# Casting loads for chunk 0's q and v and all of chunk 1, masks spread by VectorE, and preparation steps one slot later, in a fused attention and MLP kernel

## The chip, the cores and the metric

The kernel runs on one core of one Trainium2 chip. The metric is the device time of one execution in microseconds (us), lower is better. TensorE (PE) multiplies, VectorE (DVE) and ScalarE (ACT) work elementwise and empty PSUM, GpSimd (POOL) builds masks, casts, and issues the DMAs that convert types on the way, SyncE (SP) issues plain DMAs.

## What is computed

Causal attention over 4 batches, 8 heads, 768 positions, head size 64. Heads 0, 2 and 6 see all earlier positions; the others see the first 4 positions (the sinks) and the last 64. Its output, with the heads side by side, goes through a two-layer MLP.

```python
stream_keep = causal & (is_sink | in_win)
mask = np.where(retr, full_mask, stream_mask)
scores = np.where(mask, scale * np.matmul(q, k.transpose(0, 1, 3, 2)), -1e9)
a = softmax(scores)
x = np.matmul(a, v).transpose(0, 2, 1, 3).reshape(B * S, H * D)   # 3072 x 512
h = x @ w_in                                                      # 512 x 2048
out = np.maximum(0.01 * h, h) @ w_out                             # 2048 x 512
```

## The kernel before

The 3072 token rows are cut into eight **chunks** of 384, two for each batch. Every chunk n goes through four stages:

- **Load**: q, k and v as bf16, `qb`, `kb`, `va`. `load(n)` does this with casting DMAs from POOL's queue, three for each of q, k and v (one for each 128 tokens, 1024 pieces of 64 numbers). Chunk 0 and chunk 1's q and k are instead staged as fp32 in tiles `f` by `load_wide` and cast by an engine; a piece there is three tokens of a head, so that tokens come out in the order 3p+g, and the copies behind the transposes put them back (`WIDE = 2`).
- **Preparation** (`prep_pair(n, p)` for a pair p of heads, `prep_half` in chunk 0): six PE transposes into one PSUM bank, two copies to `kt` (on DVE), one to `qt`.
- **Attention** (`Attention(n)`): eight heads, each a score step (`qk`: PE, exp on ACT, mask on DVE) and a value step (`av`), then `finish` (DVE, to `xs`) and `x_t` (PE transposes through the bank `pt`, ACT copy to `xt`). Heads with a window read values shifted by 64 positions, `vb`: in chunk 0's first batch made on PE (`v_shift_pe`), otherwise by two SBUF copies by DMA (`v_shift`, L184, L185).
- **MLP**: sixteen input ticks (`in_slots`: four matmuls of 384 columns, L452, and an activation on ACT) and sixteen output slots (`out_slots`: three tiles of 128 tokens, L465, a DVE copy L470 and an output DMA from SP).

The order on every engine is that of the program text (`manual_schedule`). `merge` spreads one list of steps among another: the MLP of chunk n runs among the attention of n+1 and the preparation of n+2. `Attention.slots` hangs a preparation step (`extra`) behind the slot in which a pair's `x_t` runs. The prologue is written out by hand: constants, chunk 0's preparation and attention, chunk 1's preparation, then the first input ticks; `v_shift(3)` is issued from ACT's queue behind the MLP of chunk 1.

PSUM has eight banks: `ph`, `psS` and `po` two each, `py` and `pt` one each. POOL's DMAs use eight semaphores in turn, so an issue waits until the eighth before it has landed; POOL's other work waits behind it.

Of the kernel before, what the change touches and what calls it, by code (L numbers as in the profile page):

```python
# [21 lines left out]
def kernel(  # L22
# [46 lines left out]
    def load_wide(n, nm, half, eng):  # L69

        if half != 1:
            stage[nm, n] = rot.tile([128, 3 * H * D], FP32, name="f", tag="f", bufs=5)
            if nm != "v":
                cast[nm, n] = rot.tile([128, 3, H, D], BF16, name=f"{nm}b", tag=f"{nm}b", bufs=2)
        t = stage[nm, n]
        if nm == "v":
            for g in range(3):
                eng.dma_start(out=v_src(n)[:, g], in_=nat[nm][0, n, :, :, g])
            return
        hs = slice(0, H) if half is None else slice(4 * half, 4 * half + 4)  # L80
        eng.dma_start(out=t.rearrange("p (h x) -> p h x", h=H)[:, hs], in_=wide[nm][0, n, :, hs])

    def qk_src(nm, n):
        return stage[nm, n].rearrange("p (h g d) -> p g h d", h=H, g=3)

    def v_src(n):
        return stage["v", n].rearrange("p (g h d) -> p g h d", g=3, h=H)
# [49 lines left out]
    def zeros(i):  # L137
        nc.vector.memset(kt[i][64:128, :, 0, :], 0.0)
        nc.vector.memset(kt[i][0:64, :, 1, :], 0.0)
        nc.gpsimd.memset(va[i][:, :, :, D], 1.0)  # L140
        nc.gpsimd.memset(ksink[i][:], 0.0)
        nc.gpsimd.memset(vs[i][:, 0, :], 0.0)

    def constants():
        make_identity(nc, ident)
# [2 lines left out]
        nc.gpsimd.memset(m_win[:], 1.0)
        keep(m_win[:], [[0, 6], [-1, 64]], ALU.is_gt, 0, 1)
        keep(m_win[:], [[0, 6], [1, 64]], ALU.is_ge, 64, -1)  # L150

        nc.gpsimd.memset(shift[:], 0.0)
        nc.gpsimd.memset(e_sink[:], 0.0)
        zeros(0)
# [347 lines left out]
    constants()  # L502
    ktb, qtb = cast["k", 0], cast["q", 0]
    lo, hi = slice(0, 4), slice(4, 8)
    k0, q0, v0 = qk_src("k", 0), qk_src("q", 0), v_src(0)
# [21 lines left out]
    load_wide(1, "k", None, nc.gpsimd)
    load_wide(1, "q", None, nc.gpsimd)
    sink_mask()
    nc.gpsimd.tensor_copy(va[0][:, 0, :, 0:D], v0[:, 0])  # L530
    nc.gpsimd.tensor_copy(va[0][:, 2, :, 0:D], v0[:, 2])
    for i in range(4):
        load_w("in", i)
    load(1, "v")
    for i in range(4):
        load_w("out", i)
# [97 lines left out]
```

## Time and profile before

| what | value |
|---|---|
| median of three runs (lowest to highest) | 277.66 us (277.31 to 278.5) |
| the profiled execution: its time / its span from the first to the last instruction | 277.87 / 276.2 us |
| PE busy | 239.3 us, 87% |
| DVE, ACT, POOL busy | 112.9, 140.1, 69.9 us |

PE is busy for 87% of the span, but not evenly: the page's slices show it near full behind the first third and with holes before it. So the profile is read by stretch: when PE stood still, and who released it. The timeline gives each instruction's start and length and, in brackets, the idle time before it with the engine that ended it; the waits are the same idle times summed by the two lines.

### The profile page before, as it was taken

The page shows a single profiled execution, that of the slowest core. Times are in us where ns is not written, and L with a number is a line of the kernel's source. Part 1 is how long each engine was busy: PE and PEld are TensorE (multiplying, and loading weights), DVE is VectorE, ACT ScalarE, POOL GpSimd, SP SyncE. Part 2 cuts the span into 40 slices and gives each one's busy share as a digit, 9 for nine tenths or more (in the row PEclk, how much of TensorE's full clock was granted, in tenths as well). Part 3 has the DMA queues.
Part 4 walks back from the last instruction along what each step waited for, and adds up shares of the span by engine and source line. Part 5 has one row for each costly group of instructions (what it writes and reads, how often), then busy time and mean ns, then how long its engine had stood idle before and what let it go on. Part 6 is the DMA issues. An engine that isn't in the chain of part 4 may idle for free.

```text
span 276.2 us, 5264 instructions
## 1 busy us (share of the span) xinstructions
PE 239.3 (87%) x2135; PEld 147.3 (53%) x2164; DVE 112.9 (41%) x303; ACT 140.1 (51%) x304; POOL 69.9 (25%) x101
## 2 busy tenths in 40 slices
PE   1661669988869988979999999999999999999995
PEld 1451435545446545655666566665665566555544
DVE  6772351135363554454354524553563124311012
ACT  3652157744537327765555466655554766633300
POOL 5693936710056047009100820000000000000000
PEclk9998599999999999999999999999999999999999
DMA  6899999991249139909901992102110211011122
GB/s 215 192 250 206 188 220 160 149 101 40 77 28 143 43 55 168 84 2 93 125 34 40 96 168 44 40 4 75 38 42 29 69 38 40 0 40 39 38 78 76
DMA packets 73865, 24.63 MB, mean 89 GB/s; under 512 B 63249, under 2 KB 69649, under 8 KB 73841
## 3 DMA queue, kind: packets, MB, share of 16 engines
q0 software_dynamic: 63888, 13.24, 56.8%
q1 hardware_dynamic: 9152, 9.32, 10.4%
q10 hardware_dynamic: 800, 1.73, 2.5%
q8 instruction: 17, 0.28, 0.5%
q14 instruction: 8, 0.06, 0.1%
HBM read 27.26 MB, written 6.29 MB: 122 GB/s over the span
## 4 chain that ended last, share of the span: by engine, by line
PE 72%; DMA 9%; DVE 8%; POOL 4%; ACT 3%; issue 2%; SPq 0%; ACTq 0%; DVEq 0%
PE ph L452 26%; PE py L465 26%; PE po L287 5%; DMA w_in_bf<-in_moe_w_in_dram 4%; PE psS L329 4%; DVE kt L230 3%; PE psS L465 3%; PE pt L220 3%; DMA f<-in_k_dram 3%; DMA vb<-va 3%; PE pt L405 2%; DVE o L470 2%; PE psS L365 2%; PE psS L309 1%; DVE qt L230 1%
## 5 line engine op out<-in xcount | busy, mean ns | idle before, releaser
L452 PE MATMUL ph<-xt,w_in_bf 128*128 128x384 bf16 x512 | 102.8, 327 | 2.6 <-ACT xt L406 1.6
L454 ACT ACTIVATE g<-ph 128x384 bf16<-128x384 f32 x128 | 62.7, 491 | 61.3 <-PE ph L452 61.0
L465 PE MATMUL py<-w_out_bf,g 128*128 128x512 bf16 (+1 forms) x324 | 86.9, 373 | 3.7 <-DVE o L470 2.2
L452 PEld LDWEIGHTS <-w_in_bf 128*128 128x128 bf16 x512 | 45.6, 98 | 30.2 <-issue 4.1
L465 PEld LDWEIGHTS <-g 128*128 128x128 bf16 x400 | 35.3, 97 | 27.6 <-issue 4.0
L334 ACT ACTIVATE at<-psS 128x384 bf16<-128x384 f32 x82 | 39.6, 490 | 15.5 <-PE psS L329 14.6
L97 POOL DMA_DIRECT2D kb<-in_k_dram x18 | 15.8, 890 | 72.9 <-PE pt L220 72.5
L470 DVE COPY o<-py 128x512 f32<-128x512 f32 (+1 forms) x22 | 14.9, 678 | 32.2 <-PE py L465 32.1
L329 PE MATMUL psS<-qt,kt 128*128 128x384 bf16 (+2 forms) x105 | 26.9, 296 | 0.0
L230 DVE COPY kt<-pt 64x384 bf16<-64x384 bf16 x48 | 17.0, 355 | 18.3 <-PE pt L220 17.7
L374 DVE TENSOR_TENSOR ats<-ats,m_win 128x384 bf16<-128x384 bf16 x40 | 14.6, 365 | 20.3 <-ACT ats L370 20.0
L370 ACT ACTIVATE ats<-psS 128x384 bf16<-128x384 f32 x37 | 18.0, 490 | 9.6 <-PE psS L365 9.6
L340 DVE TENSOR_TENSOR at<-at,m_caus 128x128 bf16<-128x128 bf16 x24 | 5.4, 225 | 39.2 <-ACT at L334 39.1
L406 ACT ACTIVATE xt<-pt 128x384 bf16<-128x384 bf16 x31 | 15.2, 489 | 11.3 <-PE pt L405 10.8
L287 PE MATMUL po<-va,at 128*128 128x65 bf16 x237 | 20.0, 196 | 0.6 <-DVE at L338 0.4
L287 PEld LDWEIGHTS <-at 128*128 128x128 bf16 x252 | 16.3, 100 | 6.4 <-DVE at L338 1.0
L97 POOL DMA_DIRECT2D va<-in_v_dram x21 | 18.7, 927 | 3.0 <-DMA w_out_bf<-in_moe_w_out_dram 2.9
L399 DVE TENSOR_TENSOR xs<-po,linv 128x384 bf16<-128x384 f32 x31 | 17.3, 558 | 1.1
L97 POOL DMA_DIRECT2D qb<-in_q_dram x18 | 15.9, 910 | 4.1 <-DMA w_out_bf<-in_moe_w_out_dram 3.5
L220 PEld LDWEIGHTS <-kb 128*128 128x128 bf16 x84 | 7.0, 101 | 17.5 <-POOL kb L539 7.9
L365 PEld LDWEIGHTS <-kt 128*128 128x128 bf16 x240 | 12.5, 102 | 5.3
L287 PEld LDWEIGHTS <-ats 128*128 128x128 bf16 x240 | 11.6, 98 | 5.5 <-issue 1.8
(104 smaller groups left out, 221.6 us busy)
## 6 DMA issues: line engine op xcount, KB each, us to landing
out_dram<-o SPq DMA_DIRECT2D x23, 256.0 KB, 2.0
va<-in_v_dram POOLq DMA_DIRECT2D x21, 128.0 KB, 7.7
kb<-in_k_dram POOLq DMA_DIRECT2D x18, 128.0 KB, 4.8
qb<-in_q_dram POOLq DMA_DIRECT2D x18, 128.0 KB, 6.8
w_in_bf<-in_moe_w_in_dram POOLq DMA_DIRECT2D x4, 512.0 KB, 9.6
w_out_bf<-in_moe_w_out_dram POOLq DMA_DIRECT2D x4, 512.0 KB, 16.3
vb<-va ACTq DMA_DIRECT2D x6, 195.0 KB, 6.2
f<-in_k_dram SPq DMA_DIRECT2D x2, 384.0 KB, 5.3
```

The lines of the kernel that those rows point to most:

```text
L97: nc.gpsimd.dma_start(out=o, in_=nat[nm][b, c, :, :, g])
L230: nc.vector.tensor_copy(dst, src)
L287: nc.tensor.matmul(o, lhsT=lhsT, rhs=rhs, start=first, stop=False, skip_group_check=True)
L329: nc.tensor.matmul(s[:, off : off + w], lhsT=kt[i][:, p, hh, 128 * kj : 128 * kj + 128], rhs=qts[n][:, p, lo:CH], start=(j == 0), stop=(j ...
L334: nc.scalar.activation(out=a[:, 0:off], in_=s[:, 0:off], func=ACTF.Exp, scale=SM)
L365: nc.tensor.matmul(s[:, 64 * m : 64 * m + 64], lhsT=kt[i][:, p, hh, k0 : k0 + 128], rhs=qts[n][:, p, 64 * m : 64 * m + 64], start=(m == 0) ...
L370: nc.scalar.activation(out=av_, in_=s[:, 0:CH].rearrange("p (j e f) -> p j e f", j=3, e=2), func=ACTF.Exp, scale=SM)
L399: nc.vector.tensor_tensor(xs[:], po[:, :, :, 0:D], linv.to_broadcast([128, 3, 2, D]), op=ALU.mult)
L452: nc.tensor.matmul(ph[:, 0:CH], lhsT=w_in_bf[:, g, 128 * t : 128 * t + 128], rhs=xts[n][:, g, :], start=(g == 0), stop=(g == KG - 1))
L454: nc.scalar.activation(out=gs[n][:, t, :], in_=ph[:, 0:CH], func=ACTF.Prelu, alpha=0.01)
L465: nc.tensor.matmul(py[n][:, 0 : c1 - c0], lhsT=gs[n][:, ng, 128 * tt : 128 * tt + 128], rhs=w_out_bf[:, ng, c0:c1], start=(ng == 0), stop= ...
L470: nc.vector.tensor_copy(o[:, 0 : c1 - c0], py[n][:, 0 : c1 - c0])
```

## The change

- `load_wide` is gone. Chunk 0's k still comes as fp32, from SP in two halves (`load_k0`); chunk 0's q and v and all of chunk 1 come by `load`, in POOL's queue ahead of the weights. POOL's casts go, and so do ACT's casts of q; the second half of chunk 0's k is cast on ACT instead of on POOL. With `WIDE = 1` the copies of chunk 1's preparation are plain (both orders now put the same tokens in the same columns).
- POOL builds the window mask and the sink mask at 64 and 8 columns (`m_w`, `m_h`); DVE spreads them in `late_constants`, which stands behind chunk 0's second half of the preparation now. The zero fills of `shift`, `e_sink`, `ksink` and `vs` go from POOL to DVE.
- In chunk 0, S5's scores come behind R0's value step, and R6's second score step behind `finish(1)`. Chunk 1's second and third preparation change banks; its fourth comes behind one input tick instead of two.
- An `extra` comes one slot further behind `x_t` (`LAG + 3`). Chunk 1's output tiles take the banks `py`, `ph`, `py`. `v_shift(3)` is issued from SP right behind `v_shift(2)`, with all of `load(3)` at one place.

```diff
-    WIDE = 2
+    WIDE = 1
...
-    for half in range(2):
-        load_wide(0, "k", half, nc.sync)
-        load_wide(0, "q", half, nc.sync)
-    load_wide(0, "v", None, nc.sync)
+    load_k0(0)
+    load_k0(1)
...
     def late_constants():
...
+        nc.vector.tensor_copy(m_win[:], spread(m_w[:], 6, 64))
+        nc.vector.tensor_copy(m_win0[:, 1:], spread(m_w[:], 5, 64))
...
+                nc.vector.memset(m_h[:, h : h + 1], 0.0)
+        nc.vector.tensor_copy(m_sink[:], m_h[:].rearrange("p (h o) -> p h o", o=1).to_broadcast([128, H, D + 1]))
...
         def move(e, dst, src):
-            if n < WIDE:
-
-                src = src.rearrange("p g t -> p t g")
-                dst = dst.rearrange("p (t g) -> p t g", g=3)
-            else:
-                dst = dst.rearrange("p (g t) -> p g t", g=3)
+            dst = dst.rearrange("p (g t) -> p g t", g=3)
...
-                if extra and t in (extra_at or [last[p] + LAG + 2 for p in range(4)]):
+                if extra and t in (extra_at or [last[p] + LAG + 3 for p in range(4)]):
...
+    make_identity(nc, ident)
+    load(0, "q")
+    masks()
+    for t in va:
+        nc.gpsimd.memset(t[:, :, :, D], 1.0)
+    load(0, "v")
+    nc.vector.memset(shift[:], 0.0)
+    nc.vector.memset(e_sink[:], 0.0)
+    zeros(0)
+    load(1, "kq")
     for i in range(4):
         load_w("in", i)
     load(1, "v")
     for i in range(4):
         load_w("out", i)
-    for nm in "kq":
-        for g in range(3):
-            nc.gpsimd.tensor_copy(cast[nm, 1][:, g], qk_src(nm, 1)[:, g])
...
+    qk(*R0)
+    prep_half(0, 1, ("po", "po"),
+              lambda: nc.scalar.activation(out=cast["k", 0][:, :, 4:8], in_=k0[:, :, 4:8], func=ACTF.Copy),
+              lambda: None)
     load(2)
-    load(3, "kq")
+    late_constants()
...
-    run(in0[2:12])
+    run(in0[1:11])
     zeros(1)
-    load(3, "v")
+    load(3)
...
     v_shift(2, nc.sync)
+    v_shift(3, nc.sync)
     load(4)
     in1 = in_slots(1)
-    run(in1[0:4])
-    run(merge(in1[4:] + out_slots(1), preps(2) + Attention(2).slots(preps(3))))
-    v_shift(3)
+    run(in1[0:2])
+    run(merge(in1[2:] + out_slots(1, ("py", "ph", "py")), preps(2) + Attention(2).slots(preps(3))))
```

**POOL, from the masks to chunk 2's k.** Before, with chunk 1's q and k as wide loads to `f` and their casts behind the weights' issues:

```order
L525 CAST kb<-f 128x3x256
L81 DMA f<-in_k_dram 128x8x192
L81 DMA f<-in_q_dram 128x8x192
L169 MEMSET m_sink 128x520
L134 AFFINE_SELECT m_sink<-m_sink 128x520 x2
L174 MEMSET m_sink 128x65 x3
L530 CAST va_87<-f 128x8x64
L531 CAST va_87<-f 128x8x64
L103 DMA w_in_bf<-in_moe_w_in_dram 128x4x512 x4
L97 DMA va_87<-in_v_dram 128x8x64 x3
L106 DMA w_out_bf<-in_moe_w_out_dram 128x4x512 x4
L539 CAST kb<-f 128x512 x3
```

After, from the identity on (the first `qb` is chunk 0's, the `kb` and `qb` behind `va_79` chunk 1's):

```order
L85 DMA qb<-in_q_dram 128x8x64 x3
L133 MEMSET m_caus 128x128
L120 AFFINE_SELECT m_caus<-m_caus 128x128
L135 MEMSET m_w 128x64
L120 AFFINE_SELECT m_w<-m_w 128x64 x2
L139 MEMSET m_h 128x8
L120 AFFINE_SELECT m_h<-m_h 128x8 x2
L85 DMA va_79<-in_v_dram 128x8x64 x3
L85 DMA kb<-in_k_dram 128x8x64 x3
L85 DMA qb<-in_q_dram 128x8x64 x3
L91 DMA w_in_bf<-in_moe_w_in_dram 128x4x512 x4
```

No cast is left behind the issues of `w_out_bf`, whose waits for landings POOL must sit out; chunk 1's q and k stand ahead of all weights.

**DVE, from chunk 0's second half of `kt` to the first masked window head.** Before:

```order
L261 COPY kt_85<-po 64x2x384
L210 COPY ksink_93<-kt_85 64x4
L261 COPY kt_85<-po 64x2x384
L210 COPY ksink_93<-kt_85 64x4 x2
L374 TENSOR_TENSOR ats_95<-ats_95,m_win_81 128x3x2x64
```

After:

```order
L195 COPY ksink_85<-kt_77 64x4 x2
L148 COPY shift<-ident 128x64
L149 COPY shift<-ident 128x64
L150 COPY e_sink<-ident 128x32
L152 COPY m_win<-m_w 128x384
L153 COPY m_win_73<-m_w 128x320
L154 COPY m_win_73<-m_caus 128x64
L155 MEMSET m_win_73 4x64
L158 MEMSET m_h 128x1 x3
L159 COPY m_sink<-m_h 128x520
L355 TENSOR_TENSOR ats_87<-ats_87,m_win_73 128x3x2x64
```

Eleven instructions for constants moved in between; six of them stood ahead of the first cast of k before.

**SP, around the outputs of chunk 0** (`vb1` is the second batch's shifted v; the pair of 1040 is `v_shift(2)`, the pair of 1560 `v_shift(3)`). Before:

```order
L471 DMA out_0_dram<-o_668 128x512
L471 DMA out_0_dram<-o_742 128x512
L471 DMA out_0_dram<-o_877 128x512
L184 DMA vb1_90<-va1_88 64x1040
L185 DMA vb1_90<-va1_88 64x1040
L471 DMA out_0_dram<-o_1165 128x512
```

After:

```order
L452 DMA out_0_dram<-o_871 128x512
L169 DMA vb1_82<-va1_80 64x1040
L170 DMA vb1_82<-va1_80 64x1040
L169 DMA vb1_82<-va1_80 64x1560
L170 DMA vb1_82<-va1_80 64x1560
L452 DMA out_0_dram<-o_1182 128x512
```

The pair of 1560 came from ACT's queue, where it stood behind all of chunk 1's MLP.

## Rows read from the trace of the kernel before

**Rows 1.** The page's 40 slices of 6.9 us: busy tenths of PE

```profile
PE   1661669988869988979999999999999999999995
```

**Rows 2.** Stretches: us, busy PE, PEld, DVE, ACT, POOL (instructions), granted clock, DMA

```profile
10.00:22.00 12.00, 9.14 (x109) 6.62 (x109) 8.41 (x24) 7.93 (x18) 11.45 (x18) 1.00 1.00 227
22.00:29.00 7.00, 0.16 (x3) 0.09 (x1) 0.59 (x2) 0.49 (x1) 2.99 (x5) 0.72 1.40 199
29.00:41.00 12.00, 8.15 (x63) 5.50 (x64) 6.22 (x11) 4.47 (x10) 7.83 (x11) 0.74 1.38 208
...
129.00:276.20 147.20, 142.45 (x1200) 86.07 (x1219) 51.63 (x138) 75.13 (x163) 10.87 (x13) 1.00 0.39 56
```

**Rows 3.** PE's timeline: start, length, operation, in brackets the idle time before

```profile
21.73 0.34 PE L405 MATMUL py<-ident,xs 128*128 128x128 bf16 x3
28.91 0.29 PE L220 MATMUL ph<-ident,kb 128*128 128x128 bf16 x1 [6.84 <-POOL kb L539]
...
31.67 0.29 PE L220 MATMUL ph<-ident,qb 128*128 128x128 bf16 x1 [0.27 <-POOL qb L539]
...
40.63 1.46 PE L452 MATMUL ph<-xt,w_in_bf 128*128 128x384 bf16 x8 [0.88 <-ACT g L454]
...
53.97 1.03 PE L465 MATMUL py<-w_out_bf,g 128*128 128x512 bf16 x4
```

**Rows 4.** POOL's timeline: constants, and issues of the weights' loads

```profile
1.08 0.29 POOL masks.py:199 TENSOR_SCALAR_AFFINE_SELECT ident<-ident 128x128 bf16<-128x128 bf16 x1
...
4.47 0.16 POOL L142 MEMSET vs<- 128x65 bf16 x1
...
15.25 3.02 POOL L103 DMA_DIRECT2D w_in_bf<-in_moe_w_in_dram  x4
...
27.50 0.74 POOL L106 DMA_DIRECT2D w_out_bf<-in_moe_w_out_dram  x1 [1.76 <-DMA w_in_bf<-in_moe_w_in_dram]
```

**Rows 5.** PE's waits: us in total, times, longest

```profile
PE pt L220 <- DVE qt L230: 3.3, 4, 0.9
PE py L465 <- DVE o L470: 2.2, 4, 0.6
...
PE po L287 <- DMA vb<-va: 1.5, 1, 1.5
...
PE pt L405 <- DVE qt L230: 0.7, 1, 0.7
```

**Rows 6.** Tile kb in 78:84 us, chunk 4's casting loads: issue in ns, landing

```profile
L97 POOL DMA_DIRECT2D kb<-in_k_dram x3: 878/893/903, 79.2 to 80.9; - x3
...
DMA to landing us min/median/max: 3.4/4.3/4.4
```

**Rows 7.** ACT's timeline in chunk 0: a cast and an exp

```profile
10.15 0.84 ACT L522 ACTIVATE qb<-f 128x768 bf16<-128x768 f32 x1 [2.08 <-DMA f<-in_q_dram]
10.90 0.47 ACT L334 ACTIVATE at<-ph 128x384 bf16<-128x384 f32 x1
```

**Rows 8.** DVE's timeline from the constants to chunk 1's preparation

```profile
4.25 0.52 DVE L159 COPY m_win<-m_win 128x320 bf16<-128x320 bf16 x1
...
13.26 0.96 DVE L261 COPY kt<-po 64x768 bf16<-64x768 bf16 x1
14.26 0.57 DVE L210 COPY ksink<-kt 64x4 bf16<-64x4 bf16 x2
...
22.07 0.56 DVE L399 TENSOR_TENSOR xs<-po,linv 128x384 bf16<-128x384 f32 x1
32.00 1.12 DVE L230 COPY kt<-ph 64x384 bf16<-64x384 bf16 x2 [9.37 <-PE ph L220]
```

**Rows 9.** The page's groups: copies to kt in chunks 2 to 7

```profile
L230 DVE COPY kt<-pt 64x384 bf16<-64x384 bf16 x48 | 17.0, 355 | 18.3 <-PE pt L220 17.7
```

**Rows 10.** Tile w_out_bf in 0:75 us: from issue to landing

```profile
DMA to landing us min/median/max: 14.0/16.3/16.7
```

**Rows 11.** Tile vb in 95:125 us: chunk 3's shift of v on ACT's queue

```profile
L184 ACTq DMA_DIRECT2D vb<-va x1: 512/512/512, 103.0 to 103.0; - x1
```

More of the change, by code (lines that the diff above doesn't have):

```diff
@@ L57, in bank @@
         return ps.tile(shape, dtype, name=tag, tag=tag, bufs=BANKS[tag])
-    wide = {nm: ap.rearrange("b h (c p g) d -> b c p h (g d)", g=3, p=128) for nm, ap in (("q", q), ("k", k))}
+    kw = k[0, :, 0:CH].rearrange("h (p g) d -> p h (g d)", g=3)
     nat = {nm: ap.rearrange("b h (c g p) d -> b c p h g d", g=3, p=128) for nm, ap in (("q", q), ("k", k), ("v", v))}
@@ L67, with load_k0 @@
     cast = {}
[L69 to L76, printed above, removed]
-            for g in range(3):
[L78 to L87, printed above, removed]
+    def load_k0(half):
+        if half == 0:
+            stage["k"] = rot.tile([128, H, 3 * D], FP32, name="f", tag="f", bufs=1)
+            cast["k", 0] = rot.tile([128, 3, H, D], BF16, name="kb", tag="kb", bufs=2)
+        hs = slice(4 * half, 4 * half + 4)
+        nc.sync.dma_start(out=stage["k"][:, hs], in_=kw[:, hs])
     def load(n, nms="kqv"):
@@ L139, in zeros, with masks, spread @@
         nc.vector.memset(kt[i][0:64, :, 1, :], 0.0)
[L140 to L145, printed above, removed]
+        nc.vector.memset(ksink[i][:], 0.0)
+        nc.vector.memset(vs[i][:, 0, :], 0.0)
+    m_w = bf("m_w", 64)
+    m_h = bf("m_h", H)
+    def masks():
         nc.gpsimd.memset(m_caus[:], 1.0)
         keep(m_caus[:], [[1, 128]], ALU.is_ge, 0, -1)
[L148 to L154, printed above, removed]
+        nc.gpsimd.memset(m_w[:], 1.0)
+        keep(m_w[:], [[-1, 64]], ALU.is_gt, 0, 1)
+        keep(m_w[:], [[1, 64]], ALU.is_ge, 64, -1)
+        nc.gpsimd.memset(m_h[:], 1.0)
+        keep(m_h[:], [[-NS, H]], ALU.is_ge, 0, 1)
+        keep(m_h[:], [[NS, H]], ALU.is_ge, NS - 1, -1)
+    def spread(ap, n, w):
+        return ap.rearrange("p (o r) -> p o r", o=1).to_broadcast([128, n, w])
     def late_constants():
@@ L253, in prep_half @@
                     nc.tensor.transpose(pt[:, e, g, :], cast[nm, n][:, g, 2 * p : 2 * p + 2, :], ident[:])
+            if nm == "q":
+                nc.scalar.activation(out=qts[n][:, ps2, :].rearrange("p e (g t) -> p e g t", g=3),
+                                     in_=pt[:, :, 0:3, :], func=ACTF.Copy)
+                continue
             src = pt[:, :, 0:3, :].rearrange("p e g t -> p e t g")
             tok = lambda ap: ap.rearrange("p e (t g) -> p e t g", g=3)
-            if nm == "q":
-                nc.scalar.activation(out=tok(qts[n][:, ps2, :]), in_=src, func=ACTF.Copy)
-                continue
             for hh in range(2):
@@ L499, in preps @@
         return [lambda p=p: prep_pair(n, p) for p in range(4)]
[L502 to L505, printed above, removed]
+    make_identity(nc, ident)
[8 more added lines that the diff above has]
+    load(1, "kq")
+    for i in range(4):
+        load_w("in", i)
+    load(1, "v")
+    for i in range(4):
+        load_w("out", i)
+    k0 = stage["k"].rearrange("p h (g d) -> p g h d", g=3)
     a0 = Attention(0, ("psS", "ph"))
@@ L514, in av @@
         run([x[1] for x in us])
-    late_constants()
     prep_half(0, 0, ("pt", "py"),
-              lambda: nc.vector.tensor_copy(ktb[:, :, lo], k0[:, :, lo]),
-              lambda: nc.scalar.activation(out=qtb[:, :, lo], in_=q0[:, :, lo], func=ACTF.Copy))
+              lambda: nc.vector.tensor_copy(cast["k", 0][:, :, 0:4], k0[:, :, 0:4]), lambda: None)
     for a in ats:
         nc.vector.memset(a[:, :, 1:3, :], 0.0)
-    nc.scalar.activation(out=qtb[:, :, hi], in_=q0[:, :, hi], func=ACTF.Copy)
     qk(*R0)
     prep_half(0, 1, ("po", "po"),
-              lambda: nc.gpsimd.tensor_copy(ktb[:, :, hi], k0[:, :, hi]),
+              lambda: nc.scalar.activation(out=cast["k", 0][:, :, 4:8], in_=k0[:, :, 4:8], func=ACTF.Copy),
               lambda: None)
[L527 to L536, printed above, removed]
-    for nm in "kq":
-        for g in range(3):
-            nc.gpsimd.tensor_copy(cast[nm, 1][:, g], qk_src(nm, 1)[:, g])
     load(2)
-    load(3, "kq")
+    late_constants()
     qk(*S1, *R2, *S3)
     a0.sink(values=False)
-    nc.scalar.activation(out=va[0][:, 1, :, 0:D], in_=v0[:, 1], func=ACTF.Copy)
-    qk(*S4, *S5)
+    qk(*S4)
     v_shift_pe()
     av(*R0)
-    qk(R6[0])
+    qk(*S5)
     a0.sink_values()
@@ L551 @@
     xs0 = a0.finish(0)
-    qk(R6[1])
+    qk(R6[0])
     av(*R2)
@@ L566 @@
     a0.x_t(2, xs2, "pt")
-    prep_pair(1, 1, "ph", "vva")
-    prep_pair(1, 2, "py", "vva")
+    prep_pair(1, 1, "py", "vva")
     a0.x_t(3, xs3, "pt")
+    prep_pair(1, 2, "ph", "vva")
     v_shift(1, nc.sync)
     in0 = in_slots(0)
-    run(in0[0:2])
+    run(in0[0:1])
     prep_pair(1, 3, "py", "vva")
-    run(in0[2:12])
+    run(in0[1:11])
     zeros(1)
-    load(3, "v")
+    load(3)
     a1 = Attention(1, po_tags=("po", "po", "po", "ph")).slots(order=[0, 2, 6, 1, 3, 4, 5, 7])
-    run(merge(in0[12:] + out_slots(0), a1))
+    run(merge(in0[11:] + out_slots(0), a1))
     v_shift(2, nc.sync)
+    v_shift(3, nc.sync)
     load(4)
     in1 = in_slots(1)
-    run(in1[0:4])
-    run(merge(in1[4:] + out_slots(1), preps(2) + Attention(2).slots(preps(3))))
-    v_shift(3)
+    run(in1[0:2])
+    run(merge(in1[2:] + out_slots(1, ("py", "ph", "py")), preps(2) + Attention(2).slots(preps(3))))
     outs = []
```

14 lines of the change are left out of this document (3 added, 11 removed).

## The prediction

> **What bounds the kernel now.** I read the page's slices first [rows 1]: from the sixteenth slice on PE is mostly at nine tenths, to the end, and before that there is one deep hole in slices 4 and 5. The stretches size it [rows 2]: behind 129 us PE works 142.45 of 147.2 us, so little can be won there but by less matmul work, and none is removed. In 22 to 29 us it works 0.16 us of 7. PE's timeline says why [rows 3]: chunk 0's attention hands over at 21.73, and the first transpose of chunk 1's preparation waits 6.84 us, until 28.91, for a cast of k on POOL. POOL was not casting all that time: the casts stand in its queue behind four issues of `w_out_bf`, which sit out landings of `w_in_bf`, the last until 27.50 [rows 4]. Then the six casts set PE's pace until 31.67 + 0.29 = 31.96, and the input ticks run closed up from 40.63 [rows 3]. The waits give what is left later [rows 5]: 3.3 us for preparation steps, 2.2 us where an output tile waits for its predecessor's copy out of `py`, 1.5 us for shifted v, 0.7 us on the bank `pt`.
>
> So the number to find is when tick 4 (40.63 before) starts in the changed kernel. Everything behind it is a queue of work on PE that moves with it, less the small waits.
>
> **Part 1, POOL and its loads.** POOL has the identity at 1.08 + 0.29 = 1.37 [rows 4]; three loads of q at 0.89 each [rows 6] are issued by 4.0. The masks I put at 2.0 us: all constants behind the identity took it from 1.37 to 4.63 before [rows 4], with several times the columns. Then v is issued by 8.7, chunk 1's k by 11.4 and q by 14.1. A casting load lands 3.4 to 4.4 us after its issue [rows 6], so chunk 1's last q is there at 13.2 + 4.4 = 17.6. `w_in_bf` is issued from 14.1, where it was 15.25 [rows 4], with v and `w_out_bf` behind it as before: the weights come a good 1 us earlier, perhaps 3, since chunk 1's loads are out of their way earlier too.
>
> What this costs is chunk 0's q. Before, it came as fp32 in two halves, and PE began with the first; now both halves need all three loads. The third is issued at 3.1 and by the same row lands at 6.5 to 7.5. But it shares the DMA engines with chunk 0's k, and before, the second half of q was there only at 10.1: ACT's cast waited for it until 10.15 [rows 7]. Between 6.5 and 10.1 I take 8.5.
>
> **Part 2, chunk 0.** Six transposes and the copy of q (as the cast of the same size, 0.84 [rows 7]) bring R0's scores to 10.2, and two exps of 0.47 on ACT end at 11.5. There the cast of the second half of k stands, 0.84 again: 12.3. It was POOL's and done beside ACT's work; its cover is gone, and half 1 of the preparation waits for it. Transposes, then DVE: two copies of 0.96 and the sink keys of 0.57 [rows 8], done at 15.6; before, at 14.83. Now the moved constants, which ran ahead of the first cast before and cost nothing. A copy of 320 columns takes 0.52 with what it waits in the pipe [rows 8]; three spread copies (384, 320, 520 columns) and eight small instructions are worth 1.5 to 2.5 us, and I take 1.9: 17.5. Queued behind are the window masks; ACT's exps for these heads end at 16.4, so DVE is the late one. Its later work in chunk 0 had pauses, which take up part of this: I follow its queue (masks, shifted v, S5's mask, sink values, three normalisations) to 24.0 for the third `xs`, which ended at 22.63 [rows 8]. Chunk 0 is 1.4 us later, and PE gets to chunk 1's first transposes at 21.73 + 1.4 = 23.1. q and k lie there.
>
> **Part 3, chunk 1's preparation.** Its first pair ends at 23.1 + 0.5 = 23.6 instead of 31.96. From there to tick 4 it was 8.7 us [rows 3]. Now the kt copies are plain, 0.355 [rows 9] where they were 0.56 [rows 8]: eight on DVE, six of them on the path, 1.2 us. PE also ran at half its clock for part of this stretch: the granted clock averages 0.72 and 0.74 in 22 to 41 us [rows 2], a mix of its two levels, 2.4 and 1.2 GHz, having fallen with the hole. With no hole I take it as full. In steps: the first pair's copies (0.71) from 24.0 and a normalisation (0.76), two more pairs' copies (1.4) with PE's transposes between, 26.9; ACT's last `xt`, 27.2; tick 0, then the fourth pair (transposes, 0.71 on DVE, 0.5 on ACT) while `ph` holds two ticks, so that ticks 1 to 3 go at ACT's pace until 30.2. Tick 4 at 30.2 instead of 40.63: **10.4 us**. Each us by which q lands otherwise than at 8.5 goes into this one to one.
>
> What is late next? The fifth slot of the first output tile needs the last `w_out_bf`. That was issued at 27.50 [rows 4] and landed 16.3 to 16.7 us later [rows 10], at 44; its slot came at 53.97 [rows 3] and comes at 43.6 now. With the weights 1 to 3 us earlier they land at 41 to 43. The cover is thin, but what it can cost is 44 - 43.6 = 0.4 us as long as the weights are no later than before. Chunk 2's k and q follow the weights by 0.9 us a load, until about 47, and are wanted at 62.
>
> **Part 4, the later steps.** `v_shift(3)` behind `v_shift(2)` on SP, at about 60 instead of 103 [rows 11], needs only chunk 3's v, which is loaded by then: 1.5 us gone [rows 5]. Queued behind it on SP are chunk 1's outputs, which come 20 us later. The banks `py`, `ph`, `py` take the two waits of chunk 1's tiles, half of four that cost 2.2 [rows 5]: 1.0. The extra a slot later parts `x_t` from the transposes that want the same bank; of the 0.7 us there [rows 5] I take 0.5, since a wait may only move. The 3.3 us of preparation steps stay: DVE's three copies are the longer side with 1.25 as with 1.17 MLP steps between them. Where PE is full, a step's place costs nothing.
>
> **Sum**, against the profiled execution's own 277.87 us (its span 276.2; the median is 277.66): 10.4 + 1.5 + 1.0 + 0.5 = 13.4, so 264.5 us.
>
> **The rivals.** *(a) The clock stays low.* In chunk 0's tail PE works in pieces, and the clock may be half when the ticks start. Before, half clock held for 2 x 0.26 x 12 = 6.2 us of the stretch from 29 to 41 [rows 2], with PE at work again. As long a time from 27 on would do the work of 3.1 us: 267.6. Against it: no hole goes ahead.
>
> *(b) Chunk 0 is longer.* q at 10.1 and 2.5 us for the constants: 1.6 + 0.6 = 2.2, or 4 if the pauses on DVE take up nothing: 266.7 to 268.5.
>
> *(c) Better.* q at 6.5 (2.0), all of `pt` (0.2) and the constants at 1.5 (0.4): 261.9.
>
> *(d) The other side: POOL's issues are slowed by DVE.* The change puts fills and copies on DVE just when POOL must issue twelve casting loads in a row. If an issue took I us, the twelfth would land at 1.4 + 2.0 + 12 I + 2.5. The gain is gone when PE gets to chunk 1 at 23.1 + 13.4 = 36.5, that is at I = 2.55; at 3.0 it is 283 us. Against it: with DVE busy 8.41 of 12 us [rows 2] four issues of `w_in_bf` took 3.02, or 0.755 each, and in the quiet at 27.50 one of `w_out_bf` took 0.74 [rows 4]. The Trainium skill has a rule that speaks for this rival (SBUF — State Buffer, "SBUF: two separate sides"): a copy on VectorE in a two-port mode locks GpSimd out of the port through which it writes descriptors, so that its DMAs wait for the copy's end. The same page ("A bandwidth-pool intuition that's wrong") has a DMA of 620 ns stretched to 3100; an estimate by that factor makes an issue 4.4 us and the kernel some 300 us. The rows above do not show it, at least not with what DVE ran then.
>
> *(e) It does not do what it says:* chunk 1's k and q, in narrow pieces, land no earlier than they are wanted. By [rows 6] they have 5.5 us to spare, so this has hardly a chance of its own.
>
> **How the numbers follow.** Forecast, 0.60: 264.5, by itself 262.5 to 266.5. (a) 0.13: 267.6. (b) 0.10: 266.7 to 268.5. (c) 0.10: 261.9. (d) 0.05, of it 0.03 slower than before and the rest a lost part. (e) and other losses 0.02. The range takes in (a) to (c), with 0.4 for the weights and a little below (c) for preparation steps that get better: 261.0 to 269.0. A difference under 0.5% is about what cannot be told from no change here. Faster 0.94, same 0.02, slower 0.04.
>
> **What would show it.** Right: no wait of PE on POOL's casts; tick 4 at 29 to 32; the clock full from there; the third normalisation of chunk 0 ending at 24 to 25; `vb` out of PE's waits; two of the four `py` waits left. Wrong: PE waiting for `qb` beyond 10; issues on POOL over 1.5 us; the first output tile waiting for `w_out_bf`; a granted clock of 0.7 in 25 to 35 us.

## The result, and the profile after

The changed kernel takes 264.38 us, the median of four runs (264.2 to 265.19), beside 277.52 us for the kernel before in the same session (277.31 to 278.5, four runs): a ratio of 0.9525 with a 95% interval of 0.9495 to 0.9556. That is 13.1 us faster; the prediction was 264.5 in 261.0 to 269.0. The profiled execution took 264.29 us, its span 262.6, so 13.58 us less than the profiled execution of before. The size depends on the set: run again beside the kernel before, the pair read 264.83 and 276.02 us, 11.2 us apart (a ratio of 0.9589, 0.9552 to 0.9625). What follows reads single executions, the 13.58 among them.

The page's slices of PE, then its granted clock:

```profile
PE   1477898986999999799999999899999999999994
...
PEclk9999999999999999999999999999999999999999
```

The hole in slices 4 and 5 of [rows 1] is gone. The same stretches as in [rows 2], with the same columns (us, busy PE, PEld, DVE, ACT, POOL, granted clock, DMA):

```profile
10.00:22.00 12.00, 7.64 (x93) 5.47 (x93) 8.88 (x32) 6.33 (x16) 11.41 (x14) 1.00 1.81 154
22.00:29.00 7.00, 5.71 (x76) 4.21 (x77) 5.56 (x18) 4.71 (x12) 2.23 (x3) 1.00 1.35 201
29.00:41.00 12.00, 11.59 (x84) 6.82 (x84) 3.22 (x6) 9.80 (x23) 5.27 (x6) 1.00 1.42 213
```

In 22 to 29 us PE works 5.71 us where it worked 0.16, and in 29 to 41 it works 11.59 where it worked 8.15. What it pays is ahead of that: 7.64 instead of 9.14 in 10 to 22. PE's timeline tells the same at the places of [rows 3]:

```profile
8.64 0.61 PE L233 MATMUL py<-ident,qb 128*128 128x128 bf16 x4 [0.54 <-DMA qb<-in_q_dram]
10.15 0.48 PE L310 MATMUL ph<-qt,kt 128*128 128x384 bf16 x1 [0.90 <-ACT qt L235]
12.32 0.82 PE L233 MATMUL po<-ident,kb 128*128 128x128 bf16 x6 [1.37 <-ACT kb L515]
...
22.96 0.33 PE L205 MATMUL ph<-ident,kb 128*128 128x128 bf16 x3
...
29.43 5.63 PE L433 MATMUL ph<-xt,w_in_bf 128*128 128x384 bf16 x32 [0.36 <-ACT g L435]
...
44.04 1.02 PE L446 MATMUL py<-w_out_bf,g 128*128 128x512 bf16 x4 [0.39 <-DMA w_out_bf<-in_moe_w_out_dram]
```

The last load of chunk 0's q lets PE go on at 8.64; chunk 1's first transposes, at 28.91 before, are at 22.96 with nothing to wait for. The 32 matmuls from 29.43 on are ticks 3 to 10, so tick 4 begins four matmuls in, at 29.43 + 4 x 0.16 = 30.1, where it was 40.63. The last row is the fifth slot of the first output tile, at 53.97 before: it is 9.93 us earlier, and waits 0.39 us for the last piece of `w_out_bf`. PE's waits after, the counterpart of [rows 5] (us in total, times, longest):

```profile
PE pt L205 <- DVE qt L210: 2.6, 4, 0.9
PE pt L386 <- DVE qt L210: 2.2, 3, 0.9
...
PE po L268 <- DVE ats L355: 1.5, 3, 0.8
...
PE py L446 <- DVE o L451: 0.4, 2, 0.3
PE py L446 <- DMA w_out_bf<-in_moe_w_out_dram: 0.4, 1, 0.4
```

The waits for shifted v (`vb` by DMA) are gone, those for the output tiles' copies fall from 2.2 to 0.4. But `x_t` (L386) waits 2.2 us for the bank `pt`, where it waited 0.7.

### The profile page after: what moved, and what is told of

It is laid out like the page before. It is cut to its first block, busy times and chain, and to the rows that moved or that the text cites. A ratio compares the mean times of both kernels' runs of the same rounds, so it can differ in the third digit from the quotient of the medians.

```text
span 262.6 us, 5257 instructions
## 1 busy us (share of the span) xinstructions
PE 235.3 (90%) x2135; PEld 145.0 (55%) x2164; DVE 113.4 (43%) x314; ACT 138.3 (53%) x302; POOL 69.7 (27%) x93
## 4 chain that ended last, share of the span: by engine, by line
PE 73%; DMA 10%; DVE 6%; POOL 6%; issue 3%; ACT 1%; POOLq 0%
PE py L446 25%; PE ph L433 24%; DMA w_out_bf<-in_moe_w_out_dram 6%; PE po L268 5%; PE psS L310 4%; DMA w_in_bf<-in_moe_w_in_dram 4%; PE pt L205 3%; PE psS L446 3%; PE pt L386 2%; DVE kt L210 2%; POOL qb L85 2%; PE psS L346 2%; PE psS L290 1%; DVE qt L210 1%; DVE o L451 1%
## 5 line engine op out<-in xcount | busy, mean ns | idle before, releaser
L446 PE MATMUL py<-w_out_bf,g 128*128 128x512 bf16 (+1 forms) x309 | 82.5, 373 | 2.4 <-DVE o L451 0.4
L315 ACT ACTIVATE at<-psS 128x384 bf16<-128x384 f32 x81 | 39.1, 491 | 13.2 <-PE psS L310 12.3
L85 POOL DMA_DIRECT2D kb<-in_k_dram x21 | 18.4, 889 | 62.8 <-PE pt L205 60.3
L451 DVE COPY o<-py 128x512 f32<-128x512 f32 (+1 forms) x21 | 14.2, 678 | 32.9 <-PE py L446 32.9
L85 POOL DMA_DIRECT2D qb<-in_q_dram x24 | 21.3, 913 | 4.4 <-DMA w_out_bf<-in_moe_w_out_dram 4.0
L387 ACT ACTIVATE xt<-pt 128x384 bf16<-128x384 bf16 x31 | 15.2, 490 | 13.8 <-PE pt L386 13.3
L85 POOL DMA_DIRECT2D va<-in_v_dram x24 | 21.4, 924 | 3.7 <-DMA w_out_bf<-in_moe_w_out_dram 2.9
L355 DVE TENSOR_TENSOR ats<-ats,m_win 128x384 bf16<-128x384 bf16 x40 | 14.1, 356 | 16.4 <-ACT ats L351 15.8
L310 PEld LDWEIGHTS <-kt 128*128 128x128 bf16 x108 | 10.4, 100 | 8.3 <-issue 1.4
L346 PEld LDWEIGHTS <-kt 128*128 128x128 bf16 x240 | 12.2, 100 | 5.0
```

What stands on the lines that cost most here:

```text
L85: nc.gpsimd.dma_start(out=o, in_=nat[nm][b, c, :, :, g])
L310: nc.tensor.matmul(s[:, off : off + w], lhsT=kt[i][:, p, hh, 128 * kj : 128 * kj + 128], rhs=qts[n][:, p, lo:CH], start=(j == 0), stop=(j ...
L315: nc.scalar.activation(out=a[:, 0:off], in_=s[:, 0:off], func=ACTF.Exp, scale=SM)
L346: nc.tensor.matmul(s[:, 64 * m : 64 * m + 64], lhsT=kt[i][:, p, hh, k0 : k0 + 128], rhs=qts[n][:, p, 64 * m : 64 * m + 64], start=(m == 0) ...
L446: nc.tensor.matmul(py[n][:, 0 : c1 - c0], lhsT=gs[n][:, ng, 128 * tt : 128 * tt + 128], rhs=w_out_bf[:, ng, c0:c1], start=(ng == 0), stop= ...
L451: nc.vector.tensor_copy(o[:, 0 : c1 - c0], py[n][:, 0 : c1 - c0])
```

## The experiments

Four parts act behind the front of the kernel, each worth little, and the front differs from one execution to the next by 1 us and more. So beside the medians I read one mark in each trace: the start of the fifth slot of the first output tile (the first row with four output matmuls, x4). Up to it is the front; from it to the end of the span is the rest.

| kernel | median, us | mark | span | mark to end |
|---|---|---|---|---|
| before | 277.52 | 53.97 | 276.2 | 222.2 |
| after | 264.38 | 44.04 | 262.6 | 218.6 |
| after, run again (a_same) | 264.83 | 45.40 | 263.9 | 218.5 |
| a_front | 266.54 | 43.92 | 264.4 | 220.5 |
| a_lag2 | 263.89 | 44.31 | 262.3 | 218.0 |
| a_vs3late | 266.1 | 43.87 | 263.3 | 219.4 |
| a_py | 266.57 | 44.86 | 264.7 | 219.8 |
| a_constearly | 265.12 | 44.45 | 263.0 | 218.6 |
| a_ce_lag2 | 263.8 | 44.42 | 261.8 | 217.4 |
| b_castfirst | 268.69 | 45.12 | 267.4 | 222.3 |
| b_cf_later | 266.92 | 46.57 | 267.0 | 220.4 |
| a_qlate | 266.35 | 45.52 | 264.1 | 218.6 |
| a_best | 266.83 | 44.87 | 266.5 | 221.6 |
| a_best_act | 263.04 | 43.42 | 260.8 | 217.4 |

The last column repeats to 0.1 us where the rest of the kernel is the same: 218.6, 218.5, 218.6 and 218.6 in after, a_same, a_constearly and a_qlate, whose fronts differ by 1.5 us. The kernel before was run beside each of the three sets: 276.46, 276.02 and 275.78 us.

### The three later edits, taken out together: a_front

```diff
-                if extra and t in (extra_at or [last[p] + LAG + 3 for p in range(4)]):
+                if extra and t in (extra_at or [last[p] + LAG + 2 for p in range(4)]):
...
-    v_shift(3, nc.sync)
...
-    run(merge(in1[2:] + out_slots(1, ("py", "ph", "py")), preps(2) + Attention(2).slots(preps(3))))
+    run(merge(in1[2:] + out_slots(1), preps(2) + Attention(2).slots(preps(3))))
+    v_shift(3)
```

> The changed kernel with its three later parts undone: extra steps one slot behind as before (LAG + 2), chunk 1's output tiles all in py, v_shift(3) on ACT's queue behind chunk 1's MLP. Theory A (the prediction's sum): the front alone is worth 10.4 us, so 267.1 to 267.6 us, tick 4 at 30.1 us and the waits on vb, py and pt as in the kernel before (1.5, 2.2, 0.7 us). Rival B: the later waits only move when their cause goes, the front is worth nearly all: 264.5 to 265.5 us.

266.54 us, a ratio of 0.9645 (0.96 to 0.9691): between the two theories. The front is that of after (mark at 43.92), so the front alone carries 53.97 - 43.92 = 10.05 us. But the rest, 220.5, is 1.7 us shorter than before's 222.2, and none of the three edits is in it. What is left of the change there are the proportions in which the steps are merged (`in0[11:]`, `in1[2:]`), and smaller moves, such as chunk 3's loads at one place and fills that went from POOL to DVE. Waits of a_front:

```profile
PE pt L205 <- DVE qt L210: 2.6, 4, 0.9
PE py L446 <- DVE o L451: 1.8, 4, 0.8
...
PE po L268 <- DMA vb<-va: 1.3, 1, 1.3
```

Against [rows 5] they are 0.7, 0.4 and 0.2 us shorter, 1.3 of the 1.7; another 0.3 is a wait of `x_t` for `xs` that before has at 64.60 and a_front does not have. No kernel has the proportions alone, so that they are the cause is argued from these rows, not shown.

### One later edit undone at a time: a_lag2, a_vs3late, a_py

a_lag2 undoes the slot of the extra:

```diff
-                if extra and t in (extra_at or [last[p] + LAG + 3 for p in range(4)]):
+                if extra and t in (extra_at or [last[p] + LAG + 2 for p in range(4)]):
```

> The changed kernel with only LAG + 3 back to LAG + 2. Theory A (the prediction's term): the extra slot saves 0.5 us on the bank pt, so this is 264.9 us, slower than the changed kernel. Rival B (from the changed kernel's trace, where PE's wait of x_t's transposes for DVE's qt copies out of pt is 2.2 us and a wait for window masks 1.1 us is new): the extra slot sets the preparation right in front of the next x_t and costs 1 us or more, so this is 262.8 to 263.6 us, and the pt waits are 0.7 to 1.2 us again.

263.89 us (0.9508 to 0.9587 of before): not slower without the later slot, and its rest is 218.0, 0.6 shorter than after's, though shifted v costs it 0.4 again. The theory that the later slot is a gain falls; the rival, that the wait only moves and grows, holds. Its waits at the places in question:

```profile
PE pt L205 <- DVE qt L210: 2.6, 4, 0.9
...
PE pt L386 <- DVE xs L380: 0.8, 2, 0.6
...
PE pt L386 <- DVE qt L210: 0.7, 1, 0.7
PE po L268 <- DMA vb<-va: 0.4, 1, 0.4
```

`x_t` waits 0.7 + 0.8 us where it waits 2.2 + 0.2 in after. After's timeline at one of the three places shows why:

```profile
105.88 0.33 PE L205 MATMUL pt<-ident,kb 128*128 128x128 bf16 x3
...
107.55 0.36 DVE L210 COPY qt<-pt 128x384 bf16<-128x384 bf16 x1
107.96 0.17 PEld L386 LDWEIGHTS <-xs 128*128 128x128 bf16 x3 [1.32 <-DVE qt L210]
107.97 0.34 PE L386 MATMUL pt<-ident,xs 128*128 128x128 bf16 x3 [0.94 <-DVE qt L210]
```

A step one slot further behind its own `x_t` stands close ahead of the next pair's. It takes `pt` at 105.88, DVE empties it until 107.91, and the next `x_t` stands there. The rows of `x_t` are not all of it: value steps wait for DVE's window masks 0.34 us at 102.75 and 0.78 at 111.59 in after, where DVE has copies out of `pt` ahead of them (until 102.30 and 111.15), and in a_lag2 only 0.18, at 111.65.

a_vs3late puts `v_shift(3)` back:

```diff
-    v_shift(3, nc.sync)
...
     run(merge(in1[2:] + out_slots(1, ("py", "ph", "py")), preps(2) + Attention(2).slots(preps(3))))
+    v_shift(3)
```

> The changed kernel with only v_shift(3) back on ACT's queue behind chunk 1's MLP. Theory A: PE's wait for vb comes back at about 97 us, 1.5 us, so 265.9 us; the two copies take 6 us to land again, since chunk 5's loads go out at the same time. Rival B: the loads lie otherwise now, the copies land in 2 to 3 us and PE does not wait: 264.4 us.

266.1 us (0.9579 to 0.9691 of before), and the rest is 0.8 longer than after's (219.4 against 218.6). The wait is back, with 0.7 where theory A put 1.5:

```profile
97.17 0.19 PE L268 MATMUL po<-vb,ats 128*128 128x65 bf16 x1 [0.74 <-DMA vb<-va]
```

a_py puts chunk 1's tiles back into `py`:

```diff
-    run(merge(in1[2:] + out_slots(1, ("py", "ph", "py")), preps(2) + Attention(2).slots(preps(3))))
+    run(merge(in1[2:] + out_slots(1), preps(2) + Attention(2).slots(preps(3))))
```

> The changed kernel with only chunk 1's output tiles back in py, py, py. Theory A: two waits of 0.5 us for DVE's copy out of py, 265.4 us. Rival B: the whole fall of py's waits in the trace (2.2 to 0.4 us) is due to the banks, 266.2 us. Rival C: the waits stand beside other work and nothing moves, 264.4 us.

266.57 us, which taken alone would speak for theory B. But 0.8 us of it lie in the front (a mark at 44.86 against 44.04), which the edit does not touch. The rest is 1.2 longer than after's, and the wait for the tiles' copies is back:

```profile
PE py L446 <- DVE o L451: 1.4, 4, 0.8
```

So the bank is worth 1.2, against 1.4 - 0.4 = 1.0 in the waits, nearer to theory A's two waits of 0.5. Together, from a_front to a_lag2, both edits bring 220.5 - 218.0 = 2.5 us, and 266.54 - 263.89 = 2.65 by the medians of one set.

### Is the front bound by DVE's constants or by the weights? a_same, a_constearly, a_ce_lag2

a_same is the changed kernel again, for comparison in one set.

> The changed kernel once more, beside the ones of this call: 264.4 us by every theory.

264.83 us. a_constearly moves DVE's spread copies ahead of chunk 0's first scores, where DVE has time:

```diff
+    late_constants()
     qk(*R0)
...
     load(2)
-    late_constants()
```

> The changed kernel with late_constants ahead of R0's scores, in DVE's idle time before the second half of kt. Theory A: DVE's constants (2.3 us in the changed kernel's trace) lie on chunk 0's path, so tick 3 comes 1.0 to 1.8 us sooner than 29.4 us; but the last w_out_bf still lands at 44.0 us, where the first output tile already waits 0.4 us for it, so that this wait grows to 1.4 to 2.2 us and the time stays at 264.0 to 264.5 us. Rival B: the weights are no bound (only 0.4 us once), the gain goes through: 262.6 to 263.4 us. Rival C: chunk 0 waits for other things than the constants, tick 3 stays at 29.4 us, 264.4 us.

265.12 us: no gain. Yet the ticks are 29.43 - 28.27 = 1.2 us earlier than in after:

```profile
28.27 5.63 PE L433 MATMUL ph<-xt,w_in_bf 128*128 128x384 bf16 x32 [0.36 <-ACT g L435]
...
41.87 0.38 PE L446 MATMUL py<-w_out_bf,g 128*128 128x512 bf16 x1 [0.75 <-DMA w_out_bf<-in_moe_w_out_dram]
...
44.45 1.02 PE L446 MATMUL py<-w_out_bf,g 128*128 128x512 bf16 x4 [1.05 <-DMA w_out_bf<-in_moe_w_out_dram]
```

All of it, and more, is given back in two waits for `w_out_bf`, 1.8 us, and the mark is at 44.45. Behind the front stands a second bound, the landing of the weights at 44, and after has all but reached it. a_ce_lag2 is this kernel with `LAG + 2`, the edit of a_lag2 added.

> The changed kernel with late_constants early, as in a_constearly, and with LAG + 2. Theory A: only LAG + 2 counts, 1.1 us between tick 3 and the end, 263.3 us. Rival B: both count, 261.9 to 262.3 us.

263.8 us. The mark stays (44.42), and the rest is 218.6 - 217.4 = 1.2 shorter, 1.32 by the medians. So the later slot costs 0.6 to 1.2 us; in a_lag2, which has the 0.6, the 0.4 for shifted v stands against it, and a_ce_lag2 has no such wait.

### Is it the casting loads, or the casts' place in POOL's queue? b_castfirst, b_cf_later

The kernel before, with nothing changed but one block: its six casts ahead of the issues of `w_out_bf`.

```diff
     load(1, "v")
-    for i in range(4):
-        load_w("out", i)
     for nm in "kq":
         for g in range(3):
             nc.gpsimd.tensor_copy(cast[nm, 1][:, g], qk_src(nm, 1)[:, g])
+    for i in range(4):
+        load_w("out", i)
```

> The kernel before with one block moved: POOL's six casts of chunk 1's k and q stand ahead of the four issues of w_out_bf instead of behind them. The loads are as before. Theory A (the prediction's reading of the hole): the casts waited for nothing but their place in POOL's queue; they run from 20.9 to 24.4 us, PE's wait of 6.84 us falls to under 1 us and its preparation of the first pair ends at about 24.6 instead of 32.0 us: 269 to 271 us, and the clock's fall in 25 to 35 us is short or gone. Rival B: the hole only moves, because the weights come late or the clock is as slow: 275 to 277 us.

268.69 us, a ratio of 0.9744 (0.9694 to 0.9793): 7.3 us of the change's 11.2 in this set (276.02 - 264.83), from one moved block. POOL, then PE:

```profile
18.54 1.79 POOL L537 CAST kb<-f 128x512 bf16<-128x512 f32 x3
20.20 1.98 POOL L537 CAST qb<-f 128x512 bf16<-128x512 f32 x3
22.14 2.24 POOL L106 DMA_DIRECT2D w_out_bf<-in_moe_w_out_dram  x3
```

```profile
21.52 0.53 PE L220 MATMUL ph<-ident,kb 128*128 128x128 bf16 x3
21.84 0.63 PE L220 MATMUL ph<-ident,qb 128*128 128x128 bf16 x3
```

The first transposes of chunk 1 are at 21.52 (28.91 before) and wait for no cast. Its mark is at 45.12, 8.85 of the 9.93 us that the change gains there; its rest is that of before, 222.3 to 222.2. So the hole was made by the place of the casts in POOL's queue, and the casting loads are one of two ways to be rid of it.

One part of theory A missed: the clock still fell. The 40 input matmuls from 28.80 on ran in part at the lower level, here from 30 to 32 us:

```profile
28.80 8.61 PE L452 MATMUL ph<-xt,w_in_bf 128*128 128x384 bf16 x40
...
30.00:32.00 2.00, 2.00 (x8) 0.93 (x7) 1.46 (x2) 1.36 (x3) 1.51 (x2) 0.50 1.24 205
```

That is 8.61 / 40 = 0.215 us each, where after's 32 took 5.63 / 32 = 0.176 at a clock of 1.00; by these numbers I estimate 1.6 us for it. And the medians of this set, 268.69 and 264.83, are 3.9 us apart, of which the rest of the two kernels makes 222.3 - 218.5 = 3.8. So no run shows that the casting loads win more than the moved block does; what the change has over b_castfirst lies behind the front.

b_cf_later adds two later edits to b_castfirst: `v_shift(3, nc.sync)` behind `v_shift(2, nc.sync)`, and `out_slots(1, ("py", "ph", "py"))`.

> The kernel before with the casts ahead of w_out_bf's issues, as b_castfirst, and two of the change's later parts: v_shift(3) on SP behind v_shift(2), and the banks py, ph, py for chunk 1's output tiles. Theory A: the later parts are independent of how chunk 1 is loaded, and two waits of 0.5 us and one of 1.7 us go: 2.7 us less than b_castfirst's 268.7, 266.0 us. Rival B: the waits only move: 267 to 268.5 us.

266.92 us. The rest is 222.3 - 220.4 = 1.9 us shorter. The tiles' waits fall to half:

```profile
PE py L465 <- DVE o L470: 1.1, 2, 0.6
```

The wait for shifted v at 102 us is gone, but one of 0.7 us has come at 154.8, where there was none. The profile puts it down to DVE's copy of `o`; the matmul reads `vb`, whose two DMAs, issued at 145.5 and 146.1, took 6.8 to 8.6 us to land, so the second can have come as late as 154.7. The two edits bring 1.9 here, not the 2.5 of a_lag2.

### The order on POOL: a_qlate

```diff
-    load(0, "q")
     masks()
     for t in va:
         nc.gpsimd.memset(t[:, :, :, D], 1.0)
+    load(0, "q")
```

> The changed kernel with chunk 0's q issued behind POOL's masks instead of ahead of them, 2.5 to 2.9 us later. Theory A (the prediction: each us of q's landing goes into the time one to one): 266.9 to 267.5 us. Rival B: chunk 0's path has slack elsewhere (DVE's constants, the weights), only 1 to 1.5 us of it arrive: 265.5 to 266 us.

266.35 us, between the two theories. Chunk 0's q lands at 9.55 instead of 8.60, the first scores are at 11.10 instead of 10.15, and tick 3 begins at 31.47 instead of 29.43. Of these 2.0 us 0.95 go in one to one from q; the rest goes with a stretch at about half clock:

```profile
23.00:27.00 4.00, 4.00 (x63) 3.96 (x58) 3.49 (x12) 2.36 (x6) 0.81 (x2) 0.57 1.27 207
```

At the mark 1.5 us of it are left (45.52 against 44.04), mostly since the weights are not waited for now. q was issued only 3.25 - 1.49 = 1.8 us later, because the masks and the ones of `va` take 1.9 us here and 2.9 in after (last section), and its last load landed 4.4 us after its issue, in after 5.2.

### Can the weights land sooner? a_best, a_best_act

Both are a_ce_lag2 with chunk 1's shift of v, two DMAs that SP issues at 32.6 amid the weights' landings, moved behind them. In a_best SP issues them behind the tenth of the merged MLP steps; in a_best_act ACT does, behind the eighth:

```diff
-    v_shift(1, nc.sync)
...
-    run(merge(in0[11:] + out_slots(0), a1))
+    rest = in0[11:] + out_slots(0)
+    plain = rest[7]
+
+    def and_shift():
+        plain()
+        v_shift(1, nc.scalar)
+
+    rest[7] = and_shift
+    run(merge(rest, a1))
```

> The changed kernel with late_constants early, LAG + 2, and v_shift(1) issued from SP behind the first output of chunk 0 instead of ahead of the input ticks. Theory A (the weights' landing became the bound, and v_shift(1)'s two copies hold up w_out_bf by 1.6 us): the last w_out_bf lands at 42.0 to 42.8 us, PE's waits for it fall from 1.9 to under 0.6 us, 262.2 to 262.9 us, unless the copies now land later than 50 us and PE waits for vb. Rival B: the copies do not hold up the weights, 263.8 us or, with a wait for vb, more.

266.83 us, slower than after. The weights are there without a wait, but the shift was issued at 47.2, took 6.4 to 6.6 us to land among the loads of chunks 2 and 3, and PE waited for it:

```profile
PE po L268 <- DMA vb<-va: 2.6, 2, 2.4
```

Its rest is 221.6 - 217.4 = 4.2 us longer than a_ce_lag2's, more than the 2.6. Behind the wait of 2.4, from 55 to 60 us, the granted clock is 0.66, where a_ce_lag2 reads 1.00 from 52 to 60; with PE busy at half clock for 2 x 0.34 x 5 = 3.4 us, I estimate 1.7 for it.

> As a_best, but v_shift(1) from ACT's queue behind the third output slot of chunk 0. Theory A: as a_best, with the copies landing 2 us sooner and 1.1 us of issue on ACT, which has time: 262.2 to 262.9 us. Rival B: ACT is late behind the issue, or the copies hit the last load of weights again: 263.5 to 264.5 us.

263.04 us, a ratio of 0.9526 (0.9488 to 0.9563), the lowest median here, though just outside theory A's 262.2 to 262.9; a_ce_lag2, in another set, has 263.8 with an interval that overlaps. The shift, issued at 40.8, keeps nobody waiting, and the wait for `w_out_bf` falls from 1.9 to 0.9, not under 0.6. Time from issue to landing of `w_out_bf`, in a_ce_lag2, then in a_best_act:

```profile
DMA to landing us min/median/max: 15.1/16.1/16.4
```

```profile
DMA to landing us min/median/max: 14.7/15.2/15.4
```

Two DMAs less beside them, and the weights land 1 us sooner after their issue; a_best's median is 15.0. Both kernels with the shift moved have 15.0 to 15.2, and after and a_same, which have it amid the weights, 16.0 and 16.2.

## Why the prediction was right, and where not

**The front.** Predicted 10.4 us at tick 4, measured 40.63 - 30.1 = 10.5. The steps hold one by one: q at 8.5 (8.60), R0's scores at 10.2 (10.15), the cast of k done at 12.3 (12.26), the sink keys at 15.6 (15.78), the third `xs` at 24.0 (23.89), chunk 1's first transposes at 23.1 (22.96), ACT's last `xt` at 27.2 (26.94), tick 4 at 30.2 (30.1). That q came so near to 8.5 is in part luck: 8.5 was picked between 6.5 and 10.1, and PE goes on at 8.30 in a_front and at 8.99 in a_same, where after has 8.64. DVE's rows show the constants as the late ones:

```profile
15.83 0.18 DVE L148 COPY shift<-ident 128x64 bf16<-128x64 bf16 x1
...
17.40 0.87 DVE L159 COPY m_sink<-m_h 128x520 bf16<-128x520 bf16 x1
18.19 0.34 DVE L355 TENSOR_TENSOR ats<-ats,m_win 128x384 bf16<-128x384 bf16 x1
...
23.33 0.56 DVE L380 TENSOR_TENSOR xs<-po,linv 128x384 bf16<-128x384 f32 x1
```

From the sink keys, done at 15.78, to the first window mask at 18.19 are 2.4 us, the upper part of 1.5 to 2.5, where I took 1.9; DVE's pauses took up the rest of the difference, as the step said they would in part.

**POOL, mis-sized.** From the masks' start to v's issue were 7.14 - 4.23 = 2.9 us, not 2.0:

```profile
4.23 0.45 POOL L133 MEMSET m_caus<- 128x128 bf16 x1
4.76 0.56 POOL L120 TENSOR_SCALAR_AFFINE_SELECT m_caus<-m_caus 128x128 bf16<-128x128 bf16 x1
...
7.14 2.65 POOL L85 DMA_DIRECT2D va<-in_v_dram  x3
...
14.96 3.06 POOL L91 DMA_DIRECT2D w_in_bf<-in_moe_w_in_dram  x4
...
27.94 0.74 POOL L94 DMA_DIRECT2D w_out_bf<-in_moe_w_out_dram  x1 [1.80 <-DMA w_in_bf<-in_moe_w_in_dram]
```

`w_in_bf` was issued at 14.96 instead of 14.1, 0.3 ahead of before, and the last `w_out_bf` at 27.94, where it was 27.50. "The weights come a good 1 us earlier, perhaps 3" is the step that failed: they landed at 44.00, no earlier than before. It cost no more than the bound beside it, 44 - 43.6 = 0.4, against 0.39 in the row. The first output tile waiting for `w_out_bf` was one of the prediction's own signs of being wrong, and it came. And a bound that the text called a thin cover is, by a_constearly, where the front stops: 1.2 us won on DVE were worth nothing.

**The later steps.** Predicted 3.0, measured 222.2 - 218.6 = 3.6 from the mark on. The total was near and the split was not, so the nearness is luck. Shifted v and the banks, 1.5 + 1.0, measured 2.5 together; alone, inside after, 0.8 and 1.2. The step "an extra a slot later parts `x_t` from the transposes that want the same bank", +0.5, had the wrong sign: 0.6 to 1.2 us lost. I looked at one neighbour in the bank, the pair's own `x_t`, and not at the next pair's, nor at the window masks that then stand behind DVE's copies out of `pt`. And 1.7 us of shorter waits, preparation steps among them, I had put at nothing; the sentence that they stay at 3.3 failed (2.6). "Where PE is full, a step's place costs nothing" failed with it: before's PE works 142.45 of 147.2 us behind 129 us, and in after `x_t` waits 0.94 us at 164.96, in what is that stretch there; in a_lag2 it does not. The two errors nearly cancelled. The sum goes 9.9 + 1.7 + 2.5 - 0.6 = 13.5, against 13.58 in the profiled executions; forecast were 10.4 and 3.0. It closes by construction, since its terms are differences of one chain of kernels; what each term is put down to rests on the waits.

**The rivals.** *(d)*, DVE slowing POOL's issues: it did not happen. With DVE's fills, copies and casts beside them, issues took 2.65 / 3 = 0.88 to 2.77 / 3 = 0.92 us, as [rows 6] have them, where the rival needed 2.55. In a_qlate the three issues of q, at 3.25, ran beside DVE's cast of k: they took the same 2.77, and it was the cast that took longer, 0.85 us instead of 0.62. The rule of the Trainium skill that spoke for it (SBUF — State Buffer, "SBUF: two separate sides") was not seen at work in the issues. *(a)*, the low clock: the granted clock is 1.00 in after's stretches. It did come in other executions and went with 0.8 to 1.6 us at tick 3 there, q's landing taken out (last section), not the 3.1 I gave it. "With no hole I take it as full" held for the profiled execution of after, and that is in part luck: a_front, a_same, a_qlate and b_castfirst, which have no such hole either, ran part of 20 to 33 us at the lower level. *(e)* did not happen; *(b)* and *(c)* neither: q came at 8.60, in the middle.

## What to carry to other kernels

A work queue that issues loads which must wait for landings is the wrong place behind which to put a cast that another engine needs; moving one block on it won 7.3 of 11.2 us before anything else was rebuilt, and no run shows that new loads won more at that place. Once such a hole is closed, look for the next thing that was hidden in it, here a weight landing 0.4 us behind its use, before polishing the stage ahead of it. When a step is moved away from a neighbour that shares its bank, look at who is the neighbour on the other side.

## What the runs showed of the hardware

**A granted clock of 1.00 is not proof of full speed early in the span.** In a_same the stretch from 23 to 26 us reads 1.00:

```profile
23.00:26.00 3.00, 3.00 (x49) 3.00 (x48) 2.43 (x7) 1.75 (x4) 0.74 (x2) 1.00 1.25 209
```

But three transposes there take 0.53 us, in after 0.33 (the row at 22.96 above), and successive groups start 0.32 us apart instead of 0.17:

```profile
24.90 0.53 PE L205 MATMUL ph<-ident,kb 128*128 128x128 bf16 x3
25.22 0.46 PE L205 MATMUL ph<-ident,qb 128*128 128x128 bf16 x3
```

These are the lengths of the lower level, 1.2 GHz. Both executions run chunk 0's first transposes at such lengths (six in 0.82 us at 12.32 in after); after leaves them by 16 us, a_same at 25.4. a_same's tick 3 is at 31.34, after's at 29.43, and q was 0.35 us later: 1.6 of the 1.9 us are left, which I put down to the clock. So the same kernel has fronts that far apart, and the lengths of one known form tell it where the clock's row does not.

**Half clock also comes with no long hole ahead of it.** In a_front PE works all of 22 to 25.5 us, at 0.51; in the 2 us before, at 1.00, it worked 1.29 (1.28 in after), and its longest wait since 13 us was 1.03:

```profile
22.00:25.50 3.50, 3.50 (x49) 3.42 (x46) 3.17 (x9) 2.15 (x6) 1.26 (x2) 0.51 1.25 208
```

That PE is busy does not tell that it is fast; tick 3 was at 29.86 against 29.43 in after, though q let PE go on 0.34 us sooner (8.30). Why the clock fell here and not in after, with the same waits ahead, stays open.

**The same small POOL instructions took twice as long a few microseconds later.** The fill and the select of `m_caus` took 0.45 and 0.56 us in after, behind three issues of q; in a_qlate, ahead of them, 0.20 and 0.29:

```profile
1.32 0.20 POOL L133 MEMSET m_caus<- 128x128 bf16 x1
1.59 0.29 POOL L120 TENSOR_SCALAR_AFFINE_SELECT m_caus<-m_caus 128x128 bf16<-128x128 bf16 x1
```

The smaller masks took the same in both, and the three issues of q 2.77 us in both. DVE was filling `kt` beside them in either kernel; in after it cast k beside the select too. Whether the cast or the issues ahead slowed them was not tried and stays open.
